# Twelve weight transfers in flight, sums ahead of attention, another lead order and one-bank transposes, in a linear-attention and spectral-mixing kernel

## The chip, the cores and the metric

The kernel runs on one core of a Trainium2 chip. The metric is the device time of one execution in microseconds (us); lower is better. Each version was run several times, alternating with the kernel before on the same chip, and one execution of each was profiled. Times quoted are medians of the runs. The sets of experiments ran on different chips, so between runs of different sets a comparison of the ratios to the kernel before is the safer one.

## The reference

Two stages follow one another. The first is linear attention with a feature map, for 8 batches, 8 heads, 576 positions, head size 64. The second takes its output as `x` (8 x 576 x 512), multiplies the lowest 64 Fourier modes along the positions with one complex 512 x 512 matrix each, goes back, and adds a ReLU branch:

```
def phi(x):
    proj = x @ w_phi                                  # 64 -> 128
    proj = proj - max(abs(proj), axis=-1)
    return concat([exp(proj), exp(-proj)], axis=-1)
q_p, k_p = phi(q), phi(k)
kv  = einsum('bhsf,bhsd->bhfd', k_p, v);  z = sum(k_p, axis=2)
x   = (q_p @ kv) / (q_p . z + 1e-6)                   # heads merged: 8 x 576 x 512
X   = rfft(x, axis=1)[:, :64]                         # 64 modes
Y   = X * (w_r + i w_i)                               # 512 x 512 per mode, complex
u   = x + irfft(Y)
out = u + max(u @ w_ch, 0)
```

The weights `w_r` and `w_i` are 64 x 512 x 512 in float32 each, 134 MB together. They dwarf everything else that is read.

## The kernel before

The work is cut into 16 **units**: four groups `g` of two heads, and in each four pairs of batches `bp`. A unit has a `keys` part and a `queries` part. When the four units of a group are done, a quarter of the input channels is ready, and its 16 weight tiles (four modes each) can be multiplied: one `mix`, which this text calls a **sum**. A weight tile is 1 MB in SBUF, loaded as two halves of 512 KB with a cast to bf16. Weights, keys and queries are all issued from GpSimd (POOL).

The program's two PSUM pools take eight banks. The pool `two` has two tiles of two banks, the pool `one` four tiles of one bank.

```
ps2_cm = tc.tile_pool(name="ps2", bufs=2, space=PSUM)     # two(): two banks each
ps1_cm = tc.tile_pool(name="ps1", bufs=4, space=PSUM)     # one(): one bank each
pw_cm  = tc.tile_pool(name="pw", bufs=7)                  # weight tiles
pin_cm = tc.tile_pool(name="pin", bufs=2)                 # q, k, v of a unit

def transposed(src, name):            # keys and queries of a unit, nine 128 x 128 blocks
    dst = pm.tile([128, 9, 128], BF16, name=name, tag="xT")
    flat = src.rearrange("p n d -> p (n d)")
    ptr = two([128, 9, 128], BF16)
    for j in range(9):
        nc.tensor.transpose(ptr[:, j, :], flat[:, j * 128:(j + 1) * 128], ident_b)
    nc.scalar.copy(dst, ptr)
    return dst

def keys(st):
    kT = transposed(st["kb"], "kT")
    ...                               # AB = exp(+-proj) by ScalarE, mk = max|proj| by VectorE
    ...                               # ee = exp(+-mk); va = v * ee by VectorE (two instructions)
    for i in range(2):
        pk = one([128, 4, 65])
        ...                           # pk = AB^T va: the key-value products
        nc.scalar.copy(kvz[:, i], pk)

def queries(st, XT):
    qT = transposed(st["qb"], "qT")
    ...                               # AQ = exp(+-proj); numerators one <- kvz,AQ; xs; XT
```

The loop over units, where `keys` runs one unit ahead:

```
for n, u in enumerate(units):
    if n + 2 < len(units):
        st[units[n + 2]] = load(*units[n + 2])
    next_w(2 if g == 0 else 3)                  # issue weight tiles
    if n + 1 < len(units):
        keys(st[units[n + 1]])
    if n == 0:
        tables()
    queries(st.pop(u), XTb[g % 2])
    for _ in range(3):                          # sums of finished groups
        if mixq:
            key = mixq.pop(0)
            mix(*key, wts.pop(key), XTb[key[0] % 2])
    if bp == NP - 1:
        mixq += [(g, mg) for mg in range(NMG)]
```

After the units come the remaining sums, mixed with the `w_ch` products, then the output.

Of the kernel before, what the change touches and what calls it, by code (L numbers as in the profile page):

```python
# [10 lines left out]
F32 = mybir.dt.float32  # L11
BF16 = mybir.dt.bfloat16
# [7 lines left out]
DMODEL = 512  # L20
NG = 4
NP = 4
MG = 4
# [5 lines left out]
def kernel(  # L29
# [13 lines left out]
    nc = tc.nc  # L43

    const = ctx.enter_context(tc.tile_pool(name="const", bufs=1))
# [6 lines left out]
    def one(shape, dt=F32):  # L52
        return ps1.tile(shape, dt, name="one", tag="one")

    def two(shape, dt=F32):
        return ps2.tile(shape, dt, name="two", tag="two")
# [3 lines left out]
    xs = pers.tile([128, NG, NP, 18, D_], BF16, name="xs")  # L60
    yacc = pers.tile([128, NO, DMODEL], F32, name="yacc")

    XTb = [pers.tile([128, 10, B_, NMODES], BF16, name=f"XT{i}") for i in range(2)]

    pw_cm = tc.tile_pool(name="pw", bufs=7)
    pw = pw_cm.__enter__()
# [22 lines left out]
        return dict(g=g, bp=bp, qb=qb, kb=kb, vn=vn)  # L89


    wpf = const.tile([128, 128], F32, name="wpf")
    nc.sync.dma_start(wpf[0:64, :], w_phi)
    nc.sync.dma_start(wpf[64:128, :], w_phi)
# [6 lines left out]

    st = {(0, 0): load(0, 0)}

    ident_f = const.tile([128, 128], F32, name="ident_f")
    make_identity(nc, ident_f)
    ident_b = const.tile([128, 128], BF16, name="ident_b")
    nc.vector.tensor_copy(ident_b, ident_f)  # L107
    w2blk = const.tile([128, 256], BF16, name="w2blk")
    nc.vector.memset(w2blk, 0.0)
    nc.vector.tensor_copy(w2blk[0:64, 0:128], wpf[0:64, :])  # L110
    nc.vector.tensor_copy(w2blk[64:128, 128:256], wpf[64:128, :])

    CF = const.tile([128, 6, 4, 64], BF16, name="CF")
    CI = const.tile([128, 5, 128], BF16, name="CI")

# [2 lines left out]
    mf = const.tile([128, 64], F32, name="mf")  # L118
    nc.vector.tensor_copy(mf, mi)

    def sc(i):
        return yacc[:, 2 * i:2 * i + 2, :].rearrange("p a e -> p (a e)")[:, 0:640].rearrange(
            "p (c r m) -> p c r m", c=5, r=2)

    ang, rnd, csf = sc(0), sc(1), sc(2)
    nc.vector.tensor_tensor(
# [14 lines left out]
    def tables():  # L141

        nc.vector.memset(CF[:, 4:6], 0.0)
        for p0, p1, d, n in ((0, 128, 0, 4), (0, 64, 4, 1), (64, 128, 5, 1)):
            src = csf[p0:p1, min(d, 4):min(d, 4) + n]
            dst = CF[p0:p1, d:d + n]
            nc.vector.tensor_copy(dst[:, :, 0, :], src[:, :, 0, :])
            nc.vector.tensor_scalar_mul(out=dst[:, :, 1, :], in0=src[:, :, 1, :], scalar1=-1.0)
            nc.vector.tensor_copy(dst[:, :, 2, :], src[:, :, 1, :])
            nc.vector.tensor_copy(dst[:, :, 3, :], src[:, :, 0, :])  # L150

        cio = yacc[:, 6:8, :].rearrange("p a e -> p (a e)")[:, 0:640].rearrange(
            "p (c m t r) -> p c m t r", c=5, t=2, r=2)
        for r in range(2):
            for t in range(2):
                nc.vector.tensor_scalar_mul(
                    out=cio[:, :, :, t, r], in0=csf[:, :, r, 32 * t:32 * t + 32],
                    scalar1=(2.0 - 4.0 * r) / S_)
        for c in range(5):
            nc.vector.tensor_scalar_mul(  # L160
                out=cio[:, c, 0, 0, :], in0=cio[:, c, 0, 0, :], scalar1=0.5)
            pct = one([128, 128])
            nc.tensor.transpose(pct, cio[:, c].rearrange("p m t r -> p (m t r)"), ident_f)
            nc.vector.tensor_copy(CI[:, c, :], pct)

    def transposed(src, name):

        dst = pm.tile([128, 9, 128], BF16, name=name, tag="xT")
        flat = src.rearrange("p n d -> p (n d)")
        ptr = two([128, 9, 128], BF16)  # L170
        for j in range(9):
            nc.tensor.transpose(ptr[:, j, :], flat[:, j * 128:(j + 1) * 128], ident_b)  # L172
        nc.scalar.copy(dst, ptr)  # L173
        return dst

    def absmax(tT, m, by_head):

        for i in range(2):
            ps = two([128, 8, 128])
            for j in range(4):  # L180
                if by_head:
                    o = ps[:, 2 * j:2 * j + 2, :]
                else:
                    h, cc = j // 2, j % 2
                    o = ps.rearrange("p (c h) f -> p c h f", h=2)[:, 2 * cc:2 * cc + 2, h, :]
                nc.tensor.matmul(o, lhsT=tT[:, 4 * i + j, :],  # L186
                                 rhs=w2blk.rearrange("p (c f) -> p c f", c=2),
                                 start=True, stop=True)
            nc.vector.tensor_reduce(  # L189
                out=m[:, 8 * i:8 * i + 8], in_=ps, axis=AX.X, op=ALU.max,  # L190
                apply_absolute_value=True,
            )
            yield i, ps
        ps = one([128, 2, 128])
        nc.tensor.matmul(
            ps.rearrange("p h f -> p (h f)"), lhsT=tT[:, 8, :], rhs=w2blk,
            start=True, stop=True,
        )
        nc.vector.tensor_reduce(
            out=m[:, 16:18], in_=ps, axis=AX.X, op=ALU.max, apply_absolute_value=True,  # L200
        )
        yield 2, ps
# [118 lines left out]
        )  # L321


    def wload(g, mg):
        wt = pw.tile([128, 2, MG, DMODEL], BF16, name="wt", tag="wt")
        for i, w in ((0, moe_w_r), (1, moe_w_i)):
            nc.gpsimd.dma_start(  # L327
                wt[:, i],
                w[mg * MG:(mg + 1) * MG, g * 128:(g + 1) * 128, :].rearrange("m p e -> p m e"),
            )  # L330
        return wt
# [3 lines left out]
    def mix(g, mg, wt, XT):  # L335

        o, t = mg // 2, mg % 2
        if t == 0:
            pys[o] = one([128, DMODEL])
        py = pys[o]  # L340
        for i in range(2):
            s0 = 2 - 2 * t + 4 * i
            for j in range(MG):
                nc.tensor.matmul(  # L344
                    py[32 * j:32 * j + 32, :],
                    lhsT=XT[:, s0:s0 + 4, :, 32 * t + 4 * o + j].rearrange("p r b -> p (r b)"),
                    rhs=wt[:, i, j, :], start=(t == 0 and i == 0), stop=(t == 1 and i == 1),
                )
        if t == 0:
            return  # L350
        del pys[o]
        if g == 0:
            nc.scalar.copy(yacc[:, o, :], py)
        elif g < NG - 1:
            nc.vector.tensor_tensor(
                out=yacc[:, o, :], in0=py, in1=yacc[:, o, :], op=ALU.add)
        else:

            yst = pb.tile([128, DMODEL], BF16, name="yst")
            nc.vector.tensor_tensor(out=yst, in0=py, in1=yacc[:, o, :], op=ALU.add)  # L360
            nc.sync.dma_start(
                yall[16 * o:16 * o + 16], yst)
            pt = one([128, 4, 128], BF16)
            for dc in range(4):
                nc.tensor.transpose(pt[:, dc, :], yst[:, dc * 128:(dc + 1) * 128], ident_b)
            yT = pb.tile([128, 4, 128], BF16, name="yT")
            nc.scalar.copy(yT, pt)
            pz = one([128, DMODEL])
            for dc in range(4):
                nc.tensor.matmul(  # L370
                    pz, lhsT=yT[:, dc, :], rhs=wchb[:, dc, :],
                    start=(dc == 0), stop=(dc == 3))
            zst = pb.tile([128, DMODEL], BF16, name="zst")
            nc.scalar.copy(zst, pz)
            nc.sync.dma_start(
                zall[16 * o:16 * o + 16], zst)
# [20 lines left out]
    units = [(g, bp) for g in range(NG) for bp in range(NP)]  # L397
    wts = {}

    def next_w(n):  # L400
        for _ in range(n):
            if wq:
                key = wq.pop(0)
                wts[key] = wload(*key)
# [2 lines left out]
    mixq = []  # L407
    st[units[1]] = load(*units[1])
    keys(st[units[0]])
    for x in XTb:  # L410
        nc.gpsimd.memset(x[:, 0:2], 0.0)
        nc.gpsimd.memset(x[:, 4:6], 0.0)
        nc.gpsimd.memset(x[:, 8:10], 0.0)
    wchb = const.tile([128, 4, 512], BF16, name="wchb")
    for n, u in enumerate(units):
        g, bp = u
        if n + 2 < len(units):
            st[units[n + 2]] = load(*units[n + 2])
        next_w(2 if g == 0 else 3)
        if n + 1 < len(units):  # L420
            keys(st[units[n + 1]])
        if n == 0:
            tables()
        queries(st.pop(u), XTb[g % 2])
        for _ in range(3):
            if mixq:
                key = mixq.pop(0)
                mix(*key, wts.pop(key), XTb[key[0] % 2])
        if bp == NP - 1:
            mixq += [(g, mg) for mg in range(NMG)]  # L430
        if n == 8:
            nc.gpsimd.dma_start(wchb, moe_w_ch.rearrange("(dc p) e -> p dc e", p=128))
# [84 lines left out]
```

## Time and profile before

| | before |
|---|---|
| time, median of 3 runs | 548.3 us (548.01 to 554.12) |
| span of the profiled run | 550.3 us |
| busy share, PE / VectorE (DVE) / ScalarE (ACT) | 68% / 51% / 47% |
| first sum / last sum begins | 134.2 / 502.4 us |
| last attention numerators end | 360.7 us |

First, rows of the page that cut the span into 40 slices (a digit is a busy share in tenths; PEclk is the granted TensorE clock), and its line on the chain of work that ended last.

```profile
PEclk9999575775675897678975777799989996565899
DMA  9699993343999999999999999799999999995466
PE 41%; DMA 23%; ACT 18%; DVE 12%; issue 4%; POOL 2%; DVEq 0%; POOLq 0%; ACTq 0%
```

The DMA engines are busy nearly always, with one hole from the seventh to the tenth slice. The windows view has finer numbers. Its columns are the stretch in us and its length, then PE, PE weight load, DVE, ACT and POOL busy, and at the end the granted clock, the DMA share and the GB/s that landed.

```profile
83.00:135.00 52.00, 36.93 (x348) 25.32 (x355) 31.37 (x58) 30.29 (x46) 13.24 (x20) 0.66 0.36 57
135.00:345.00 210.00, 153.85 (x1528) 102.55 (x1531) 132.07 (x218) 128.03 (x198) 86.68 (x124) 0.75 1.18 191
364.00:480.00 116.00, 76.48 (x511) 34.23 (x515) 24.01 (x49) 27.21 (x47) 33.34 (x45) 0.87 1.24 210
```

A share of 1.24 is what saturation looks like in this trace. Between 83 and 135 us it is 0.36. The hole stands between two weight issues of POOL (start, duration, instruction, idle time before it and what ended that):

```profile
61.30 0.74 POOL L327 DMA_DIRECT2D wt<-in_moe_w_i_dram  x1 [0.56 <-DMA wt<-in_moe_w_i_dram]
...
135.63 0.76 POOL L327 DMA_DIRECT2D wt<-in_moe_w_r_dram  x1 [0.86 <-PE one L344]
```

The seventh tile fills the last buffer at 61 us; the eighth waits until a sum (line L344) frees one.

Two lines of the list of waits (total us, times, longest):

```profile
POOL wt L327 <- PE one L344: 37.4, 5, 17.0
PE two L172 <- ACT AB L212: 25.9, 13, 7.9
```

One of the groups of instructions (operation, tiles and shapes, count, then busy time and mean in ns, idle time before it and what ended it):

```profile
L230 PE MATMUL one<-va,AB 128*128 128x65 bf16 x512 | 48.2, 231 | 2.6 <-DVE va L219 2.6
```

### The profile page before, as it was taken

To read this page: it belongs to the slowest core of one execution; us is meant where nothing else is said; L and a number is where in the kernel's file an instruction comes from. 1 tells how busy PE (TensorE), PEld (TensorE's weight loads), DVE (VectorE), ACT (ScalarE), POOL (GpSimd) and SP (SyncE) were. 2 spreads that over 40 slices of the span, in tenths; PEclk is the share of its full clock that TensorE was granted. 3 is DMA by queue.
4 is the path that set the end of the run, shared out by engine and by line. 5 is a ranking of instruction groups with operands and counts; after the bars stand their busy time and mean duration, and the time that the engine had idled before them with its cause. 6 is when DMAs were issued, how large, how long until landed. Compare 5 with 4: busy or idle time off the path is not lost.

```text
span 550.3 us, 8008 instructions
## 1 busy us (share of the span) xinstructions
PE 376.5 (68%) x3103; PEld 221.7 (40%) x3133; DVE 279.7 (51%) x486; ACT 256.5 (47%) x403; POOL 186.8 (34%) x273
## 2 busy tenths in 40 slices
PE   2377767658667666778768677787766774345995
PEld 1255545445445444455445354343333331111342
DVE  7647485584555764566965665662222220000574
ACT  3346555655565566567665565312221331011463
POOL 8853331133432715626242533143223222200000
PEclk9999575775675897678975777799989996565899
DMA  9699993343999999999999999799999999995466
GB/s 166 87 225 204 215 140 60 64 49 65 206 189 210 135 218 178 160 213 180 214 218 215 181 181 184 117 204 206 206 206 206 212 216 213 215 213 99 163 267 267
DMA packets 112341, 98.63 MB, mean 179 GB/s; under 512 B 17968, under 2 KB 110768, under 8 KB 111280
## 3 DMA queue, kind: packets, MB, share of 16 engines
q0 software_dynamic: 94736, 77.09, 90.0%
q1 hardware_dynamic: 17568, 21.04, 12.6%
q8 instruction: 24, 0.39, 0.3%
q14 instruction: 13, 0.11, 0.1%
HBM read 163.64 MB, written 9.44 MB: 314 GB/s over the span
## 4 chain that ended last, share of the span: by engine, by line
PE 41%; DMA 23%; ACT 18%; DVE 12%; issue 4%; POOL 2%; DVEq 0%; POOLq 0%; ACTq 0%
DMA wt<-in_moe_w_i_dram 15%; DMA wt<-in_moe_w_r_dram 8%; PE two L186 7%; PE one L230 6%; ACT AQ L263 5%; PE one L236 5%; PE one L344 5%; ACT AB L211 4%; PE pt L466 3%; ACT AB L212 3%; PE one L283 3%; DVE mk L189 3%; PE one L312 3%; PE pt L468 3%; ACT qT L173 2%
## 5 line engine op out<-in xcount | busy, mean ns | idle before, releaser
L327 POOL DMA_DIRECT2D wt<-in_moe_w_r_dram x64 | 48.9, 764 | 93.3 <-PE one L344 37.4
L263 ACT ACTIVATE AQ<-two 128x1024 bf16<-128x1024 f32 x64 | 61.6, 1027 | 14.8 <-PE two L186 6.1
L327 POOL DMA_DIRECT2D wt<-in_moe_w_i_dram x64 | 49.0, 765 | 48.7 <-DMA wt<-in_moe_w_i_dram 44.7
L81 POOL DMA_DIRECT2D kb<-in_k_dram x32 | 23.6, 736 | 78.4 <-PE one L283 32.7
L394 ACT CAST xw<-one 128x512 bf16<-128x512 f32 x36 | 21.1, 585 | 62.0 <-PE one L392 54.9
L230 PE MATMUL one<-va,AB 128*128 128x65 bf16 x512 | 48.2, 231 | 2.6 <-DVE va L219 2.6
L392 PE MATMUL one<-wchb,xT 128*128 128x512 bf16 x137 | 39.7, 408 | 13.9 <-DVE xT L389 13.5
L186 PE MATMUL two<-w2blk,qT 128*128 128x256 bf16 x128 | 30.2, 386 | 26.4 <-ACT qT L173 26.3
L211 ACT ACTIVATE AB<-two 128x1024 bf16<-128x1024 f32 x32 | 32.9, 1028 | 31.4 <-DVE mk L189 24.6
L283 PE MATMUL one<-kvz,AQ 128*128 128x65 bf16 x512 | 35.2, 226 | 15.5 <-ACT AQ L263 13.8
L344 PE MATMUL one<-wt,XT_70 128*32 128x512 bf16 x256 | 28.7, 524 | 24.1 <-DMA wt<-in_moe_w_i_dram 14.4
L189 DVE TENSOR_REDUCE mk<-two 128x8 f32<-128x1024 f32 x32 | 42.1, 1493 | 4.7 <-PE two L186 4.7
L389 DVE COPY xT<-one 128x512 bf16<-128x512 bf16 x36 | 15.3, 424 | 56.4 <-PE one L387 56.3
L219 DVE TENSOR_TENSOR va<-vn,ee 128x1152 bf16<-128x1152 f32 x32 | 42.0, 1356 | 0.0
L189 DVE TENSOR_REDUCE mq<-two 128x8 f32<-128x1024 f32 x32 | 38.9, 1218 | 4.2 <-PE two L186 4.0
L283 PEld LDWEIGHTS <-AQ 128*128 128x128 bf16 x512 | 28.8, 120 | 28.4 <-ACT AQ L263 22.9
L312 PE MATMUL one<-CF,xs 128*128 128x256 bf16 x160 | 30.0, 309 | 13.1 <-DVE xs L303 12.1
L81 POOL DMA_DIRECT2D qb<-in_q_dram x32 | 23.4, 731 | 43.5 <-PE two L172 24.3
L230 PEld LDWEIGHTS <-AB 128*128 128x128 bf16 x512 | 32.4, 119 | 10.5 <-issue 3.2
L212 ACT ACTIVATE AB<-two 128x1024 bf16<-128x1024 f32 x32 | 33.0, 1032 | 0.0
L344 PE MATMUL one<-wt,XT_69 128*32 128x512 bf16 x256 | 26.5, 465 | 7.0 <-DMA wt<-in_moe_w_i_dram 5.8
L172 PE MATMUL two<-ident_b,kb 128*128 128x128 bf16 x144 | 18.1, 280 | 19.0 <-DVE ident_b L107 8.4
(136 smaller groups left out, 716.5 us busy)
## 6 DMA issues: line engine op xcount, KB each, us to landing
wt<-in_moe_w_r_dram POOLq DMA_DIRECT2D x64, 512.0 KB, 14.5
wt<-in_moe_w_i_dram POOLq DMA_DIRECT2D x64, 512.0 KB, 16.2
vn<-in_v_dram SPq DMA_DIRECT2D x32, 256.0 KB, 6.7
out_dram<-of SPq DMA_DIRECT2D x8, 1024.0 KB, 3.9
kb<-in_k_dram POOLq DMA_DIRECT2D x32, 128.0 KB, 5.5
qb<-in_q_dram POOLq DMA_DIRECT2D x32, 128.0 KB, 5.8
vn<-in_v_dram SPq DMA_DIRECT2D x32, 32.0 KB, 7.3
XT_69<-yst SPq DMA_DIRECT2D x8, 128.0 KB, 6.1
```

The source lines that it names most:

```text
L81: eng.dma_start(t[:, 8 * i:8 * i + 8, :].rearrange("p (h c) d -> p h (c d)", h=2), hs[:, 0:512, :].rearrange("h (p c) d -> p h (c d)", c=4),)
L186: nc.tensor.matmul(o, lhsT=tT[:, 4 * i + j, :], rhs=w2blk.rearrange("p (c f) -> p c f", c=2), start=True, stop=True)
L189: nc.vector.tensor_reduce(out=m[:, 8 * i:8 * i + 8], in_=ps, axis=AX.X, op=ALU.max, apply_absolute_value=True,)
L211: nc.scalar.activation(dst[:, 0], ps, ACT.Exp, scale=1.0)
L212: nc.scalar.activation(dst[:, 1], ps, ACT.Exp, scale=-1.0)
L219: nc.vector.tensor_tensor(out=va[:, ab, :, 0:64], in0=st["vn"], in1=ee[:, ab, :].unsqueeze(2).to_broadcast([128, 18, 64]), op=ALU.mult,)
L230: nc.tensor.matmul(o, lhsT=ABs[i][:, ab, 4 * h + c, :], rhs=va[:, ab, 8 * i + 4 * h + c, :], start=(c == 0), stop=False,)
L263: nc.scalar.activation(AQ[:, ab], ps, ACT.Exp, scale=1.0 - 2.0 * ab)
L283: nc.tensor.matmul(pn[ab][:, n - n0, :], lhsT=AQs[i][:, ab, c % 2, 2 * h + c // 2, :], rhs=kvz[:, i, 2 * h + ab, :], start=True, stop=True,)
L312: nc.tensor.matmul(px[:, :, i, :], lhsT=xs[:, g, bp, n:n + 2, :].rearrange("p h d -> p (h d)"), rhs=CF[:, c if c < 4 else 4 + i], start=(c ...
L327: nc.gpsimd.dma_start(wt[:, i], w[mg * MG:(mg + 1) * MG, g * 128:(g + 1) * 128, :].rearrange("m p e -> p m e"),)
L344: nc.tensor.matmul(py[32 * j:32 * j + 32, :], lhsT=XT[:, s0:s0 + 4, :, 32 * t + 4 * o + j].rearrange("p r b -> p (r b)"), rhs=wt[:, i, j, ...
```

## The change

Its intent: fill the DMA hole by holding twelve weight tiles before the first sums, five of them in memory that is not used yet; start sums ahead of a unit's attention, eight in a row the first time; start sooner (identity first, clearing moved off POOL); take transposes out of the two-bank PSUM pool; and put one exponential ahead of its reduce. In this text the parts have letters.

```
 # A: lead order
+    ident_f, ident_b made first; XTb cleared by VectorE; table scratch in xs, not yacc      (cut)
 # B: transposes in one-bank tiles
-        ptr = two([128, 9, 128], BF16)
-        for j in range(9):
-            nc.tensor.transpose(ptr[:, j, :], flat[:, j * 128:(j + 1) * 128], ident_b)
-        nc.scalar.copy(dst, ptr)
+        for lo, hi in ((0, 4), (4, 9)):
+            ptr = one([128, hi - lo, 128], BF16)
+            for j in range(lo, hi):
+                nc.tensor.transpose(ptr[:, j - lo, :], flat[:, j * 128:(j + 1) * 128], ident_b)
+            nc.scalar.copy(dst[:, lo:hi, :], ptr)
 # C: second half of the maximum: exponentials (at the yield) ahead of the reduce
+            if i == 1:
+                yield i, ps
             nc.vector.tensor_reduce(...)
-            yield i, ps
+            if i == 0:
+                yield i, ps
 # D: twelve transfers
+    def home(g, mg):      # group 0: tiles 0, 1 in yacc, 2 in XTb[1], 10 and 11 in xs, others in pw
+    next_w(2)                                          # before the loop
-        next_w(2 if g == 0 else 3)
+        next_w((3, 3, 2, 2)[n] if g == 0 else 3)
 # E: sums ahead of the unit, eight the first time
+        some(8 if n == 4 else 3)
 # F: at the last unit of a group, keys of the next unit after the queries
-        if n + 1 < len(units):
+        ahead = n + 1 < len(units)
+        if ahead and bp < NP - 1:
             keys(st[units[n + 1]])
         queries(st.pop(u), XTb[g % 2])
-        (three sums)
+        if ahead and bp == NP - 1:
+            keys(st[units[n + 1]])
```

More of the change, by code (lines that the diff above doesn't have):

```diff
@@ L89, in load @@
         return dict(g=g, bp=bp, qb=qb, kb=kb, vn=vn)
+    ident_f = const.tile([128, 128], F32, name="ident_f")
+    make_identity(nc, ident_f)
+    ident_b = const.tile([128, 128], BF16, name="ident_b")
+    nc.vector.tensor_copy(ident_b, ident_f)
     wpf = const.tile([128, 128], F32, name="wpf")
@@ L102 @@
     st = {(0, 0): load(0, 0)}
-    ident_f = const.tile([128, 128], F32, name="ident_f")
-    make_identity(nc, ident_f)
-    ident_b = const.tile([128, 128], BF16, name="ident_b")
-    nc.vector.tensor_copy(ident_b, ident_f)
     w2blk = const.tile([128, 256], BF16, name="w2blk")
@@ L111, with clear @@
     nc.vector.tensor_copy(w2blk[64:128, 128:256], wpf[64:128, :])
+    def clear(x):
+        for i in (0, 4, 8):
+            nc.vector.memset(x[:, i:i + 2], 0.0)
+    clear(XTb[0])
     CF = const.tile([128, 6, 4, 64], BF16, name="CF")
@@ L119 @@
     nc.vector.tensor_copy(mf, mi)
+    scr = xs[:, 1].rearrange("p b n d -> p (b n d)").bitcast(F32)
     def sc(i):
-        return yacc[:, 2 * i:2 * i + 2, :].rearrange("p a e -> p (a e)")[:, 0:640].rearrange(
-            "p (c r m) -> p c r m", c=5, r=2)
+        return scr[:, 640 * i:640 * i + 640].rearrange("p (c r m) -> p c r m", c=5, r=2)
     ang, rnd, csf = sc(0), sc(1), sc(2)
@@ L150, in tables @@
             nc.vector.tensor_copy(dst[:, :, 3, :], src[:, :, 0, :])
-        cio = yacc[:, 6:8, :].rearrange("p a e -> p (a e)")[:, 0:640].rearrange(
-            "p (c m t r) -> p c m t r", c=5, t=2, r=2)
+        cio = scr[:, 640:1280].rearrange("p (c m t r) -> p c m t r", c=5, t=2, r=2)
         for r in range(2):
@@ L321, in queries @@
         )
+    def home(g, mg):
+        if g == 0 and mg < 2:
+            t = yacc.bitcast(BF16).rearrange("p o e -> p (o e)")[:, 4096 * mg:4096 * mg + 4096]
+        elif g == 0 and mg == 2:
+            t = XTb[1].rearrange("p s b m -> p (s b m)")[:, 0:4096]
+        elif g == 0 and mg in (10, 11):
+            t = xs[:, mg - 8].rearrange("p b n d -> p (b n d)")[:, 0:4096]
+        else:
+            return pw.tile([128, 2, MG, DMODEL], BF16, name="wt", tag="wt")
+        return t.rearrange("p (i m e) -> p i m e", i=2, m=MG)
     def wload(g, mg):
-        wt = pw.tile([128, 2, MG, DMODEL], BF16, name="wt", tag="wt")
+        wt = home(g, mg)
         for i, w in ((0, moe_w_r), (1, moe_w_i)):
@@ L409, with some @@
     keys(st[units[0]])
-    for x in XTb:
-        nc.gpsimd.memset(x[:, 0:2], 0.0)
-        nc.gpsimd.memset(x[:, 4:6], 0.0)
-        nc.gpsimd.memset(x[:, 8:10], 0.0)
     wchb = const.tile([128, 4, 512], BF16, name="wchb")
+    def some(n):
+        for _ in range(n):
+            if mixq:
+                key = mixq.pop(0)
+                mix(*key, wts.pop(key), XTb[key[0] % 2])
+                if key == (0, 2):
+                    clear(XTb[1])
+    next_w(2)
     for n, u in enumerate(units):
@@ L424 @@
         queries(st.pop(u), XTb[g % 2])
-        for _ in range(3):
-            if mixq:
-                key = mixq.pop(0)
-                mix(*key, wts.pop(key), XTb[key[0] % 2])
+        if ahead and bp == NP - 1:
+            keys(st[units[n + 1]])
         if bp == NP - 1:
```

## The prediction

> **What bounds the kernel now.** The DMA engines, starved early. In the windows view their share is 1.24 to 1.27 when saturated (26 to 69 us, 364 to 480 us). One weight tile (a half of w_r and one of w_i, 512 KB each) then takes 5.1 us: the spacing of the POOL issues of 366 to 405 us. 64 tiles are 326 us. Between 83 and 135 us the share is 0.36, so some 37 us of DMA time are lost; 6 more at 345 to 364 us. Cause: seven tiles, all the buffers, are issued by 61 us; the eighth at 135.6 us, when the first sums (weight matmuls, 134.2 us) free a buffer. The Trainium skill, "DMA: Bandwidth & Descriptors", section "Anatomy of one DMA", says that DMA engines do not wait on semaphores, the issuing sequencer does; the trace agrees: POOL stood 12.8 and 17.0 us before weight issues near 333 and 355 us. After 364 us the chain of waits is mostly weight DMAs until the last sums at 502 us; then 48 us of output.
> Between 135 and 345 us the share is 1.18. Attention nearly co-limits: units take 20 to 21.5 us also at 50 to 113 us, without sums.
>
> **What changes.**
> 1. Twelve tiles instead of seven ahead of the sums: 5 x 5.1 = 25.5 us of transfers moved into the idle stretch.
> 2. The first sums go ahead of a unit instead of behind it, eight at once; queries of unit 3 go ahead of keys of unit 4. Sums are cheap (two tiles in 1.1 to 1.7 us). They should start at 105 to 112 us, so transfers resume some 25 us sooner, one unit's inputs (5 us) fewer being done. The eight cost PE 8 us once.
> 3. Lead: identity first, memsets off POOL: first weight issue at 13 us, not 21; first key exponential near 12 us, not 18.8 (behind a DVE reduce behind tables).
> 4. Transposes in one-bank tiles with two copies: about 0.3 us more ACT each (a copy is 1.02 us), against 25.9 us of PE waits for transposes behind exponentials. At most 1 us gained per unit.
> 5. Keys after queries at three boundaries lose overlap: 0 to 4 us each.
>
> **Sum.** Twelve tiles land by about 95 us; DMA idles until about 108. Then 52 tiles x 5.1 = 265, inputs of ten units x 5.3 = 53, 5% loss in the attention stage 12, slower last tiles (5.6 us apart after 433 us) 5: last tile about 445 us. From last landing to end, unchanged, 52 us: 497. With some loss where attention cannot hold the pace: **502 us**, 8 in 10 between 486 and 521. All of the gain is on the critical path while DMA limits.
> Chances: faster by over 2% 0.95, within 2% 0.04, slower 0.01.
>
> **What would show it.** Twelve tiles issued by 70 us; DMA share near 1.2 up to 90 us, a remaining hole under 25 us; first weight matmul at 105 to 115 us; the pure DMA stage after attention 16 to 20 tiles instead of 26; last weight issue near 430 us instead of 480; last 48 us unchanged. If attention is quicker, units fall below 20 us.
>
> **What would make it wrong.** Attention becoming the limit (boundaries, competition for one-bank PSUM tiles, lower granted clock), so that full buffers stall transfers again; weight traffic delaying key and query loads in the same queue; or attention much quicker from freed PSUM, so that transfers never pause: below 490.

## More of the kernel before

The order of instructions on an engine is not the order of the text: the tool that compiles the program reorders them.

Next, one unit in the middle, from the timeline: L172 are the transposes, L219 the making of `va`, L186 projections, L230 the key-value products.

```profile
163.61 0.66 PE L172 MATMUL two<-ident_b,qb 128*128 128x128 bf16 x9 [2.52 <-ACT AB L212]
166.26 2.63 DVE L219 TENSOR_TENSOR va<-vn,ee 128x1152 bf16<-128x1152 f32 x2
167.12 1.04 PE L186 MATMUL two<-w2blk,qT 128*128 128x256 bf16 x4 [2.85 <-ACT qT L173]
167.95 0.43 PE L230 MATMUL one<-va,AB 128*128 128x65 bf16 x4
```

While ACT and DVE prepare `va` for the next unit's keys, PE already transposes and projects this unit's queries.

## The result and the profile after

The changed kernel took 599.31 us (597.41 to 600.21, 4 runs), against 549.0 for the kernel before in the same comparison. The ratio is 1.0891, with a 95% interval of 1.0817 to 1.0966: slower by 9%, and correct. Ratios here are the mean time of one kernel's runs over that of the other's in the same rounds, so they are not quite the ratio of the quoted medians. Executions over 1.5% slower than the fastest of the same kernel are left out of the means.

The lines that answer to those of before: the two rows of the page, then the windows.

```profile
PEclk9996666756677677767677756666589999998799
DMA  9999999219994957899499929695969999998276
```

```profile
83.00:135.00 52.00, 35.93 (x319) 22.61 (x318) 26.11 (x44) 22.80 (x40) 13.89 (x21) 0.62 0.58 92
135.00:345.00 210.00, 131.40 (x1167) 82.11 (x1168) 106.99 (x177) 103.20 (x168) 73.76 (x107) 0.71 0.98 157
```

The one hole has become many. From 135 to 345 us DMA moves 157 GB/s instead of 191, and PE, DVE and ACT also do 15 to 19% less than before. So no engine became the bottleneck; something makes all of them wait. The early part went as planned: POOL issues the twelfth tile at 74.7 us. But the thirteenth again waits for a sum.

```profile
74.69 0.77 POOL L348 DMA_DIRECT2D xs<-in_moe_w_i_dram  x1
...
132.38 0.76 POOL L348 DMA_DIRECT2D wt<-in_moe_w_r_dram  x1 [16.19 <-PE one L365]
```

The list of waits names who stands still. L365 is the sum, L228 makes `va`, L239 is the key-value product, L221 an exponential of keys.

```profile
POOL wt L348 <- PE one L365: 160.8, 21, 21.5
PE one L239 <- DVE va L228: 121.5, 16, 8.4
DVE mk L197 <- ACT AB L221: 51.4, 15, 3.8
```

Once in each of the 16 units PE stands for 7.6 us on average (121.5 / 16) until `va` is there. Before, that wait was 2.6 us in total, as shown above. One unit of the timeline shows it (L178 transposes, L192 projections):

```profile
253.86 2.63 DVE L228 TENSOR_TENSOR va<-vn,ee 128x1152 bf16<-128x1152 f32 x2
255.37 0.38 PE L239 MATMUL one<-va,AB 128*128 128x65 bf16 x4 [7.52 <-DVE va L228]
...
256.34 0.72 PE L178 MATMUL one<-ident_b,qb 128*128 128x128 bf16 x5
...
259.87 0.61 PE L178 MATMUL one<-ident_b,qb 128*128 128x128 bf16 x4
260.27 2.03 PE L192 MATMUL two<-w2blk,qT 128*128 128x256 bf16 x8
```

The query transposes, which before filled this wait, now stand behind the products that wait, and PE stood for 7.52 us rather than run them first. Their data were there: the wait began at 247.9 us, the last query loads before it were issued at 219.5 us, and no query load of this trace took more than 17.8 us to land.

The compiled order of PE says the same without any run, and the traces show both orders (but for single matmuls whose records are missing). Below is one steady unit of each kernel. Tk and Tq are transposes of keys and queries, Pk, Pkr, Pq, Pqr, PQ, PQr projections, KV key-value products, N numerators, F the transform, S sums; the number counts matmuls.

```
before:  F3 Pk2 S16 Pk5 F1 Pk1 Pkr1 F6  Tq9 Pq4 KV10 Pq4 Pqr1 PQr2 KV30 PQ4 N16 Tk6 N4 Tk3 N20
after:   F3 S16 Tk9 F7 Pk8 Pkr1         KV10 Tq5 KV30 Tq4 Pq8 Pqr1 PQr2 PQ4 N40
```

Both transposes moved. Queries' went from ahead of the products into and behind them; keys' went from inside the numerators (N16 Tk6 N4 Tk3 N20) to behind all of them.

The time can be split at the last attention numerators. Before, attention ends at 360.7 us and the rest takes 189.6 us. After, attention ends at 448.9 us and the rest takes 146.7 us. So the change saves 43 us behind attention, about what was hoped for, and loses 88 us in it.

### The profile page after: what moved, and what is told of

Same layout as the page of the kernel before. It is cut to its first block, busy times and chain, and to the rows that moved or that the text cites. A ratio compares the mean times of both kernels' runs of the same rounds, so it can differ in the third digit from the quotient of the medians.

```text
span 595.6 us, 8060 instructions
## 1 busy us (share of the span) xinstructions
PE 386.8 (65%) x3133; PEld 221.7 (37%) x3133; DVE 282.8 (47%) x492; ACT 265.6 (45%) x436; POOL 181.6 (30%) x267
## 5 line engine op out<-in xcount | busy, mean ns | idle before, releaser
L239 PE MATMUL one<-va,AB 128*128 128x65 bf16 x512 | 51.4, 243 | 121.5 <-DVE va L228 121.5
L348 POOL DMA_DIRECT2D wt<-in_moe_w_r_dram x59 | 44.8, 760 | 180.0 <-PE one L365 160.8
L239 PEld LDWEIGHTS <-AB 128*128 128x128 bf16 x512 | 32.9, 123 | 134.3 <-issue 117.5
L197 DVE TENSOR_REDUCE mk<-two 128x8 f32<-128x1024 f32 x32 | 39.2, 1224 | 82.7 <-ACT AB L221 51.4
L292 PE MATMUL one<-kvz,AQ 128*128 128x65 bf16 x512 | 31.2, 211 | 32.0 <-ACT AQ L272 31.2
L348 POOL DMA_DIRECT2D wt<-in_moe_w_i_dram x59 | 45.2, 765 | 16.2 <-DMA wt<-in_moe_w_i_dram 12.2
L179 ACT COPY qT<-one 128x512 bf16<-128x512 bf16 (+1 forms) x32 | 20.0, 640 | 51.1 <-PE one L178 51.1
L228 DVE TENSOR_TENSOR va<-vn,ee 128x1152 bf16<-128x1152 f32 x32 | 42.1, 1359 | 0.0
L179 ACT COPY kT<-one 128x512 bf16<-128x512 bf16 (+1 forms) x32 | 19.6, 642 | 48.2 <-PE one L178 48.2
L292 PEld LDWEIGHTS <-AQ 128*128 128x128 bf16 x512 | 22.5, 107 | 46.0 <-ACT AQ L272 44.1
L321 PE MATMUL one<-CF,xs 128*128 128x256 bf16 x160 | 34.8, 349 | 0.6 <-DVE xs L312 0.2
L249 ACT CAST kvz<-one 128x260 bf16<-128x260 f32 x32 | 12.0, 376 | 48.8 <-PE one L245 48.8
L81 POOL DMA_DIRECT2D kb<-in_k_dram x32 | 23.7, 740 | 32.1 <-PE one L178 23.1
L221 ACT ACTIVATE AB<-two 128x1024 bf16<-128x1024 f32 x32 | 33.1, 1034 | 0.0
L365 PE MATMUL one<-wt,XT_70 128*32 128x512 bf16 x256 | 27.4, 508 | 6.0 <-DMA wt<-in_moe_w_i_dram 3.0
```

Source lines behind the costliest of these rows:

```text
L81: eng.dma_start(t[:, 8 * i:8 * i + 8, :].rearrange("p (h c) d -> p h (c d)", h=2), hs[:, 0:512, :].rearrange("h (p c) d -> p h (c d)", c=4),)
L179: nc.scalar.copy(dst[:, lo:hi, :], ptr)
L197: nc.vector.tensor_reduce(out=m[:, 8 * i:8 * i + 8], in_=ps, axis=AX.X, op=ALU.max, apply_absolute_value=True,)
L221: nc.scalar.activation(dst[:, 1], ps, ACT.Exp, scale=-1.0)
L228: nc.vector.tensor_tensor(out=va[:, ab, :, 0:64], in0=st["vn"], in1=ee[:, ab, :].unsqueeze(2).to_broadcast([128, 18, 64]), op=ALU.mult,)
L239: nc.tensor.matmul(o, lhsT=ABs[i][:, ab, 4 * h + c, :], rhs=va[:, ab, 8 * i + 4 * h + c, :], start=(c == 0), stop=False,)
```

## The experiments

The expectations speak of four theories; their letters aren't those of the parts. Theory A: part B, the one-bank transposes, costs the time through the order on PE. Its rivals are Theory B (parts E and F: sums ahead, keys after queries at group ends), Theory C (part C: the reduce behind the exponentials) and Theory D (weight traffic ahead of key and query loads, which comes of part D).

"Unit" is the time from the first unit's small query exponential (ACT writing AQr, once per unit) to the last unit's, divided by 15. "Attention" is the end of the last numerators, and "rest" the span from there. These three are of the profiled run. Two of those, marked *, were slow. The medians of these two (e3 and g3) include two slow runs each.

| run | median us | ratio to before | unit us | attention us | rest us |
|---|---|---|---|---|---|
| before | 549 | 1 | 20.8 | 361 | 190 |
| after | 599.3 | 1.089 | 26.8 | 449 | 147 |
| e1 after, two-bank transposes | 510.3 | 0.931 | 21.0 | 361 | 146 |
| e2 after, reduce first | 579.0 | 1.054 | 25.4 | 429 | 147 |
| e3 both | 514.6 | 0.929 | 21.5* | 369* | 148* |
| e4 before, one-bank transposes | 627.4 | 1.143 | 26.2 | 442 | 183 |
| f1 after, two-bank, two copies | 530.2 | 0.962 | 22.4 | 382 | 148 |
| f2 after, one-bank for keys only | 553.3 | 1.003 | 23.7 | 404 | 147 |
| f3 after, one-bank for queries only | 548.8 | 0.995 | 23.6 | 400 | 145 |
| f4 after, query transposes written first | 570.5 | 1.034 | 25.0 | 422 | 147 |
| h1 after, transposes in a bank of their own | 490.9 | 0.894 | 19.3 | 335 | 152 |
| g1 e1 with seven in flight | 516.2 | 0.940 | 21.5 | 369 | 147 |
| g2 e1 with sums behind | 522.9 | 0.952 | 20.9 | 355 | 167 |
| g3 e1 with keys ahead at group ends | 503.8 | 0.910 | 20.8* | 358* | 147* |
| i1 after, shared pool of three banks | 614.9 | 1.120 | 27.7 | 466 | 148 |
| i2 before, transposes in a bank of their own | 518.6 | 0.945 | 19.1 | 328 | 191 |
| i3 h1 with seven in flight | 500.2 | 0.910 | 19.2 | 333 | 165 |
| i4 h1 with keys ahead at group ends | 485.3 | 0.885 | 19.0 | 331 | 153 |

All 16 experiments were correct.

### First set: which part

**e1.** Part B undone, all else as in the changed kernel.

```
-        for lo, hi in ((0, 4), (4, 9)):
-            ptr = one([128, hi - lo, 128], BF16)
-            ... transposes of lo to hi, one copy each
+        ptr = two([128, 9, 128], BF16)
+        ... nine transposes, one copy
```

> The changed kernel with one part undone: the nine transposes of a unit go into one two-bank PSUM tile with one copy, as in the kernel before. Theory A (one-bank transposes put the query transposes behind the key-value products in PE's issue order; keys and queries of neighbouring units no longer overlap, units take 26 to 28 us instead of 20 to 21): units fall back to about 21 us, PE no longer waits 121 us for va, total 495 to 520 us. Theory B (the eight sums ahead of a unit and keys after queries at the group ends cost the time): stays at 585 to 600. Theory C (the exponential ahead of the reduce delays va): stays at 585 to 600. Theory D (weight traffic ahead of key and query loads): stays at 585 to 600.

Measured: 510.27 us (508.32 to 513.38), ratio 0.9309 [0.9258, 0.9361]. Units are back at 21.0 us. Part B is worth 89 us (599.3 - 510.3), and without it the rest of the change is a gain of 7%.

**e2.** Part C undone.

```
-            if i == 1:
-                yield i, ps
             nc.vector.tensor_reduce(...)
-            if i == 0:
-                yield i, ps
+            yield i, ps
```

> The changed kernel with one part undone: in the second half of a key's maximum the reduce comes ahead of the exponentials again. Theory C (the reduce behind the exponentials holds va and with it PE): units lose most of their extra 6 us, total below 530. Theory A: the query transposes are still behind the products (the issue order of PE in a unit is unchanged), a small gain of 0.5 to 1.5 us per unit, total 575 to 595.

Measured: 578.97 us, ratio 1.0541 [1.0501, 1.0581]. Part C costs 20 us in this kernel (units of 25.4 us instead of 26.8), but most of the loss stays.

**e3.** B and C undone.

> Both undone. Theory A: 490 to 515, within 10 us of the run with only the two-bank transposes. Theory C: about as the run with only the reduce first. Theory B or D: still 585 to 600.

Measured: 514.55 us (508.98 to 518.48), ratio 0.9293 [0.9232, 0.9353]. That interval overlaps e1's: with two-bank transposes part C makes no difference that these runs show. (The wait that part C brings, of VectorE's `mk` for the exponential, is still 42.5 us in e1's trace, against 51.4 us in the changed kernel.) Theory C falls as the main cause.

**e4.** The kernel before, with part B alone.

> The kernel before with the one-bank transposes alone, nothing else changed. Theory A: units of 26 to 27 us as in the changed kernel, total 610 to 640 (slower than the changed kernel, which still has its twelve early transfers). Theories B, C, D: about 549, unchanged.

Measured: 627.35 us, ratio 1.1425 [1.1382, 1.1469], units of 26.2 us. One edit of `transposed` costs the kernel before 78 us, and brings the same wait:

```profile
PE one L231 <- DVE va L220: 107.7, 16, 9.1
```

Theories B and D fall as the main cause, since none of their parts is in this kernel.

### Second set: what about the one-bank transposes

**f1.** The two-bank tile, still copied in two pieces.

```
+        pall = two([128, 9, 128], BF16)
         for lo, hi in ((0, 4), (4, 9)):
-            ptr = one([128, hi - lo, 128], BF16)
+            ptr = pall[:, lo:hi, :]
```

> The changed kernel with the transposes in one two-bank tile again, but still copied out in two pieces. In the compiled order of PE the query transposes stand ahead of the key-value products again. If the tiles and the order they lead to are the cause: 505 to 520 us, as in the first experiment (510). If the extra copies on ScalarE are the cause: 570 to 600.

Measured: 530.23 us, ratio 0.9616 [0.9545, 0.9687]. It lies between the two ranges. Copying in two pieces costs 20 us (530.2 - 510.3; 17 by the ratios), the pool the other 69 us (70 by the ratios). The compiled order changed too: the key transposes are cut in two, the second part behind the numerators (Tk4 N24 Tk3 F3 Tk2), so these 20 us are not the copies' busy time alone: two copies take 1.31 us on average where the one of e1 takes 1.16, 5 us over the 32.

**f2 and f3.** One-bank tiles for only one of the two.

```
-        for lo, hi in ((0, 4), (4, 9)):
-            ... (as in the change)
+        if name == "kT":        # f2; "qT" in f3
+            ... (as in the change)
+        else:
+            ... (as before)
```

> The changed kernel with one-bank transposes for keys only; queries use the two-bank tile. The compiled PE order has the query transposes ahead of the products. If the order is the cause: units of 20 to 22 us, total 503 to 520. If any one-bank transposes cost the time (slots shared with the products): about half of the loss stays, 540 to 570.

> The changed kernel with one-bank transposes for queries only. The compiled PE order has them behind the products. If the order is the cause: units of 25 to 28 us, PE waits over 90 us for va, total 575 to 600. If the shared slots cost the time: about half of the loss, 540 to 570.

Measured: 553.33 us for keys only (ratio 1.0026) and 548.78 us for queries only (0.9948). Against e1 that is 43 and 39 us, together 82 of the 89 (by the ratios 39 and 35, 74 of 87). The first form of Theory A, in which only the place of the query transposes counted, falls: it gave f2 503 to 520. Each of the two costs about half. From the lists of waits, first f2, then f3:

```profile
PE one L245 <- DVE va L234: 30.3, 4, 7.7
```

```profile
PE one L245 <- DVE va L234: 72.8, 12, 8.1
```

With late query transposes (f3) PE stands ahead of the products at the twelve units where queries run beside the keys. With late key transposes (f2) it stands only at the four that begin a group, where no queries run beside them. Both together give the 16 of the changed kernel. At the other units keys' cost is of another kind. Their compiled order is `N40 F3 S16 Tk9`, so the next unit's chain of transposes, exponentials and `va` starts only when all numerators are issued.

**f4.** One-bank tiles kept, query transposes written ahead of the next unit's keys.

```
+            st[u]["qT"] = transposed(st[u]["qb"], "qT")
             keys(st[units[n + 1]])
             ... (and `queries` takes qT from there)
```

> The changed kernel with its one-bank transposes kept, but the query transposes of a unit written ahead of the next unit's keys in the program (at all units but the last of a group). The compiled PE order then has query transposes and projections ahead of the products. If the order is the cause: units of 20 to 22 us, total 500 to 520, with the same tiles and the same number of copies as the slow kernel. If the one-bank tiles or the copies themselves cost the time: 580 to 600.

Measured: 570.49 us, ratio 1.0344. This missed the expectation by 50 us. The compiled order is `N40 F3 S1 F1 S15 Tq9 Tk8 F6 Tk1 Pk8 Pkr1 Pq8 PQ4 KV10`. Queries' do stand ahead of the products, but both kinds now stand behind all numerators. PE's wait for `va` falls to 49.5 us (1.6 to 1.7 us at twelve units), yet 60 us of the loss against e1 stay. So the loss is not this one wait alone, and it isn't enough for queries' transposes to be ahead of the products. Read from these orders, and not tested by itself: each transpose has a stretch in which PE would otherwise wait, and both are needed.

The granted clock does not explain the loss: f4's four runs had 0.733 to 0.751 and took 570 us, the changed kernel's 0.758 to 0.772 and 599 us.

### Third set: the pool, and the other parts

The refined theory: the transposes come late because they must get a slot (a buffer of a pool) from the pool that the products use, and these hold it.

**h1.** One-bank tiles and two copies kept, in a bank of their own.

```
-    ps1_cm = tc.tile_pool(name="ps1", bufs=4, space=bass.MemoryType.PSUM)
+    ps1_cm = tc.tile_pool(name="ps1", bufs=3, space=bass.MemoryType.PSUM)
+    pst_cm = tc.tile_pool(name="pst0", bufs=1, space=bass.MemoryType.PSUM)
...
-            ptr = one([128, hi - lo, 128], BF16)
+            ptr = pst0.tile([128, hi - lo, 128], BF16, name="tr", tag="tr")
```

> The changed kernel with one-bank transposes and two copies kept, but in a PSUM pool of their own of one bank, so that they share no slot with the products; the products' pool shrinks from four banks to three. In the compiled PE order the query transposes stand ahead of the products again. If slots shared with the products put the transposes late: most of the loss goes, 515 to 545 us (the two copies alone cost 20 us in the run with a two-bank tile, and one bank fewer for the products may cost some). If one-bank transposes cost the time whatever the pool: 580 to 600.

Measured: 490.85 us (488.0 to 492.89), ratio 0.8937 [0.888, 0.8994]. It is better than expected, and better than both kernels and e1. The wait of the products for `va` is nearly gone, 8.7 us instead of 121.5:

```profile
PE one L241 <- DVE va L230: 8.7, 6, 3.6
```

The order is as expected. Read from the trace (200.3 to 217.9 us; single records can be missing), a steady unit has both kinds of transposes ahead of the products, some of them already for the unit after:

```
h1:      F3 S5 F1 S11 Pkr1 Tq5 Pq8 Tk4 F6 Tk5 PQ1 Tq4 PQ2 Pk2 KV10 Pqr1 Pk2 KV30 PQr2 N6 Pk1 N6 Pk3 N28
```

Its chain of work that ended last, another wait, and the same window as before:

```profile
DMA 49%; PE 29%; ACT 7%; POOL 5%; DVE 5%; issue 3%; DVEq 0%; ACTq 0%; POOLq 0%
```

```profile
PE tr L180 <- DMA kb<-in_k_dram: 41.1, 8, 14.7
```

```profile
135.00:345.00 210.00, 154.46 (x1618) 101.75 (x1629) 143.31 (x247) 127.68 (x216) 89.69 (x129) 0.83 1.25 204
```

DMA is saturated (1.25) through the attention stage and has 49% of the chain, and the transposes now wait for key transfers to land. Why h1 is also 20 us better than e1 is not taken apart: its transposes have left the two-bank pool as well, and its granted clock was higher (0.844 to 0.866 against 0.787 to 0.803).

**g1.** e1 without part D.

```
-        wt = home(g, mg)
+        wt = pw.tile([128, 2, MG, DMODEL], BF16, name="wt", tag="wt")
...
-    next_w(2)
-        next_w((3, 3, 2, 2)[n] if g == 0 else 3)
+        next_w(2 if g == 0 else 3)
```

> The first experiment's kernel (two-bank transposes, 510 us) without the twelve transfers: weights use the seven buffers alone and are issued two per unit in the first group. The prediction's item 1 (five more tiles in flight are worth 5 x 5.1 = 25 us): 530 to 540. If early transfers are worth little because attention limits: 508 to 515.

Measured: 516.17 us, ratio 0.9395 [0.9331, 0.9459] against e1's 0.9309 [0.9258, 0.9361]. The intervals overlap a little; D is worth about 6 us here, not 25. The windows show where the transfers went, first g1, then e1:

```profile
60.00:120.00 60.00, 42.05 (x404) 27.15 (x405) 34.52 (x60) 36.95 (x56) 20.34 (x31) 0.74 0.72 111
120.00:360.00 240.00, 177.78 (x1666) 117.35 (x1681) 150.63 (x250) 132.28 (x206) 98.69 (x141) 0.68 1.24 203
```

```profile
60.00:120.00 60.00, 43.18 (x420) 27.84 (x417) 37.81 (x65) 35.46 (x54) 28.97 (x43) 0.72 1.18 187
120.00:360.00 240.00, 174.04 (x1704) 116.38 (x1715) 153.27 (x256) 136.61 (x212) 93.03 (x133) 0.71 1.16 189
```

Twelve in flight do fill the hole (1.18 against 0.72). But afterwards e1 runs DMA at 1.16 and g1 at 1.24: attention sets the pace, buffers are full, and what was moved early is given back later.

**g2.** e1 with the sums behind the queries.

```
-        some(8 if n == 4 else 3)
         ...
         (after queries)
+        some(8 if n == 4 else 3)
```

> The first experiment's kernel with the sums behind the queries of each unit again (eight first, then three). The prediction's item 2 (transfers resume a unit sooner): 520 to 535. If attention limits: 505 to 512.

Measured: 522.91 us, ratio 0.9524 [0.9446, 0.9601]. Sums ahead are worth 13 us. First sums begin at 124.8 us here against 103.8 us in e1, and the rest takes 167 us against 146.

**g3.** e1 with keys ahead of queries also at the group ends.

```
-        if ahead and bp < NP - 1:
+        if ahead:
             keys(st[units[n + 1]])
         queries(st.pop(u), XTb[g % 2])
-        if ahead and bp == NP - 1:
-            keys(st[units[n + 1]])
```

> The first experiment's kernel with keys ahead of queries also at the group ends. The prediction's item 5 (0 to 4 us lost at each of three ends, against sums that start later): 500 to 518, within 2% of 510.

Measured: 503.81 us (497.28 to 507.53), ratio 0.9096 [0.9012, 0.9181]. Part F costs about 2% in the two-bank kernel, at the upper end of the 0 to 12 us that item 5 allows.

### Fourth set: what was still open

**i1.** The changed kernel, shared pool, three banks: one number changed (`bufs=4` to `bufs=3`).

> The changed kernel (transposes and products share one pool) with that pool at three banks instead of four. If the bank of their own was what helped: PE order still has the query transposes behind the products, 600 to 625 us. If the smaller pool was what helped: 490 to 530.

Measured: 614.88 us, ratio 1.12. Three banks are worse than four, by 16 us; h1 gained by the bank of their own, not by the smaller pool. The trace has the query transposes behind the first products again (`KV10 Tq4 KV30 Tq5`), and the wait is back:

```profile
PE one L239 <- DVE va L228: 118.2, 16, 7.8
```

**i2.** The kernel before with the one-bank transposes in a bank of their own (the edit of h1 on top of e4).

> The kernel before with the one-bank transposes in a bank of their own and three banks for the products. If sharing of slots was the cause of the 78 us that the same transposes cost in the shared pool: 525 to 555 us. If one-bank transposes cost the time by themselves: above 600.

Measured: 518.61 us, ratio 0.9453 [0.9398, 0.9507]. It is 6 us better than the expected range. The same transposes that cost 78 us in the shared pool (627.35 against 549.2 for the kernel before in e4's set) gain 32 us in their own bank (518.61 against 550.31 in this set). Units take 19.1 us, and the rest is as long as before. The first sums begin at 111.8 us instead of 134.2, so 22 of the 32 us are gained before the first sums: attention's pace also set how long the DMA hole lasted.

**i3.** h1 without part D (the edit of g1).

> The own-bank kernel (491 us) without the twelve transfers: seven buffers alone. If item 1 of the prediction holds where transfers limit (25 us): 505 to 520. If the twelve are worth no more here than in the two-bank kernel (6 us): 493 to 500.

Measured: 500.21 us, ratio 0.91 [0.9036, 0.9163] against h1's 0.8937 [0.888, 0.8994]. So the twelve are worth 9 us here, too, far less than 25. Here attention keeps up (units of 19.2 and 19.3 us), and the rest is 165 us against 152. But the hole that the five tiles could fill was already small, as these windows show, first i3, then h1:

```profile
60.00:120.00 60.00, 46.25 (x468) 32.02 (x470) 38.42 (x67) 40.48 (x70) 24.21 (x35) 0.76 0.99 157
```

```profile
60.00:120.00 60.00, 42.38 (x448) 29.65 (x450) 40.16 (x70) 38.86 (x66) 29.68 (x43) 0.83 1.17 188
```

In i3 the first sum is at 97.8 us, so buffers come free sooner. (1.17 - 0.99) / 1.25 of 60 us is 8.6 us of DMA time, an estimate from these lines, close to the 9 us measured. Early weights have a price in h1 that was named among the risks of the prediction, "weight traffic delaying key and query loads in the same queue": PE waits for keys for 3.6, 3.6 and 4.4 us at 52, 88 and 104 us, where i3's trace has no such wait between 14 and 167 us, and h1's first sum comes 9.6 us later. That these waits make the delay is not tested.

**i4.** h1 with keys ahead at the group ends (the edit of g3).

> The own-bank kernel with keys ahead of queries also at the group ends. If attention were still the limit: 476 to 484. If transfers limit already: 485 to 495, the same within 2%.

Measured: 485.3 us (484.64 to 486.98), ratio 0.8847 [0.8787, 0.8907]. It is the fastest median, 11.5% below the kernel before, though its interval overlaps h1's.

## Why the prediction was wrong, point by point

- **The total, 502 us (486 to 521), with a chance of 0.95 of being faster by over 2%: wrong.** Measured 599.3, slower by 9%.
- **The step that failed is item 4**: "At most 1 us gained per unit" from transposes in one-bank tiles. They cost about 5.6 us per unit (89 us over 16 units). The copies' busy time was not what cost it: the two take 1.28 us in the changed kernel's trace, the one before 1.15 (not 1.02). I costed two copies against the waits for the two-bank pool, and did not look at where the transposes would land in the compiled order, although that order was there to read before the run. They now take slots from the pool that numerators and key-value products use. In the order that results, keys' transposes stand behind all numerators and queries' behind the first products (82 us of the 89 by the medians of f2 and f3). h1 shows that it's the sharing: the same tiles and copies in a bank of their own bring 490.9 us and cut the wait for `va` from 121.5 to 8.7 us, and i1 rules out the pool's size. Where they don't share, they gain 1.7 us per unit (20.8 to 19.1, i2), so even the good side of item 4 was sized too low. That slots are handed out while the order is made is inferred from these orders and runs.
- **The warning was there but had no weight.** The last paragraph names "competition for one-bank PSUM tiles" and "full buffers stall transfers again". Both happened: POOL waited 160.8 us for sums instead of 37.4. But this wait does not measure the loss: e1, which is fast, has 114.5 us of it.
- **What bounds the kernel before: half right.** The hole was there, and so was its cause. "Attention nearly co-limits" understated it: i2, which changes only the tiles and the pools of attention's transposes, gains 32 us, all of it in attention (the rest is 191 us against 190).
- **Item 1, five tiles worth 25.5 us: the mechanism right, the size wrong.** 6 us in e1's kernel, where attention gives the time back, and 9 us in h1's, where items 1 and 2 fill the same hole and can't be added, and where early weights seem to hold up key loads (i3).
- **Item 2, sums at 105 to 112 us: right to about 1 us without part B** (103.8 us in e1), 124.8 us with it. Worth 13 us by g2.
- **Item 3: right.** First weight issue at 13.5 us (13 predicted), first key exponential at 11.3 us (12 predicted). What part A is worth was not tested alone.
- **Item 5, 0 to 4 us at each of three ends: right.** In all about 2% (12 us) by the ratios of g3 and e1, the upper end; 6 us by their medians, but g3's includes two slow runs.
- **The rest of the sum was near.** Without part B it measures 510.3 us against 502, and the part from the start of the last sum to the end stayed near 48 us (46.4 in e1, 47.6 in the changed kernel). Items 1 and 2, each taken out alone, account for 6 and 13 of e1's 39 us; no run takes out both. Of the 44 us that e1 saves behind attention, g2 shows 22 to come from sums ahead. The others are argued, not tested alone: five more sums done by the end of attention spare 5 x 5.1 = 25.5 us of transfers there.

The Trainium skill points at the wait, once there is a trace of the changed kernel. "Perfetto Trace Analysis", section "Optimization Strategy" (under "Identifying Performance Opportunities"), says that a gap which repeats for a stretch, on the engine that should be saturated, can mean that there isn't enough SBUF or PSUM for the next tile to be allocated. The trace agrees in part: PE's gap of 7.6 us repeats at all 16 units and a bank of their own for the transposes all but removes it, but PE is not the engine that was saturated before, and the amount of PSUM stayed the same. The statement in "DMA: Bandwidth & Descriptors", section "Anatomy of one DMA", that waits happen on the issuing sequencer, holds after the change too: POOL stood for up to 21.5 us ahead of weight issues while DMA ran dry.

## What to carry to other kernels

When a tile moves to another PSUM pool, ask which tiles it will compete with and read the compiled order of the engine that writes it: a cheap instruction that stands behind a waiting one can no longer fill its wait, here 7.6 us in each unit. Give short-lived tiles that should run ahead a slot of their own, even at the price of a smaller pool for the others. Gains that fill the same hole don't add, and a hole filled early gives time only if the stage after it can use what came early.

## What the Trainium skill lacked or had wrong

- "PSUM — Partial Sum Buffer" has no word on what sharing one pool among short-lived and long-waiting tiles does to the order: 599.3 us with a shared pool of four banks, 614.9 with three, 490.9 with three and one apart.
- "Perfetto Trace Analysis" lists repeated gaps as a possible sign of too little SBUF or PSUM. Here the amount was the same (eight banks) in the slow and in the fast kernel; how it was divided made the 18% (490.9 against 599.3).
- "DMA: Bandwidth & Descriptors" gives no rate for loads that cast. Here tiles that land as 1 MB of bf16 from twice as many bytes came 5.1 us apart, and 210 GB/s landed between 364 and 480 us of the kernel before.
